# Attention and mixer kernel: three pairs' keys and queries sent ahead of the branch, weight parts in DRAM in rows of 2 KB, and new figures in the planner

## The chip, the cores and the metric

The kernel runs on one core of a Trainium2 chip. The metric is the device time of one execution in microseconds. The kernel before takes 676.57 us (median of three runs, 676.33 to 677.78).

## The reference

Four batches of eight heads, 768 positions, head size 64; each position attends to four sink positions and to a window of 128. The heads' outputs, joined to 512 columns, go through a low-rank mix over positions (U and V, rank 32) and a feed-forward layer of 512 to 2048 to 512 columns. U, V and the two weights are float64.

```python
scores = scale * np.matmul(q, k.transpose(0, 1, 3, 2))
keep = is_sink | in_window
scores = np.where(keep, scores, -1000000000.0)
a = np.exp(scores - np.max(scores, axis=-1, keepdims=True))
a = a / (np.sum(a, axis=-1, keepdims=True) + 1e-09)
x = np.matmul(a, v)                      # joined over the heads to (batch, 768, 512)
h = x.transpose(0, 2, 1) @ U @ V
u = x + h.transpose(0, 2, 1)
out = u + np.maximum(u @ w_ch1, 0.0) @ w_ch2
```

## The kernel before

**Order.** The class `Fast` records every piece of work as a step with an engine (or several to choose from), a duration, what it reads and writes, and a priority. `Plan.order` (L321) lays these steps out in time with a list scheduler (`forward`, L419), corrects the priorities from the end (`backward`, L382), repeats that 40 times and keeps the best order. The steps are then issued engine by engine in that order; an engine works its own list strictly in turn, and so does SP, which issues nearly all DMAs. The figures of the planner are constants at the head of the file: `SWITCH` is what it charges PE for going between matmuls on quarter or half tiles and whole ones, `LAND` the time from a DMA's data to its use, `BACKLOG` the time from which the DMA queues count as busy. No step moves during a run; a wrong figure shows as a wait.

**Beginning.** Before the branch on the window's size (`tc.If`, L1671) the kernel makes masks and constants and sends first transfers: keys (two pieces each) and the first half of the queries of `NFIRST` pairs (L1649 to L1653), and the float64 words of U, of both halves of V and of the first weight tile, into the tiles `big0` to `big3` (L1656 to L1658). `load` (L713) leaves out what is already sent, and `narrow` (L635) takes a `big` tile from the list `early` as long as there is one.

**Attention of batch 0.** Four pairs of heads, in two halves of 384 positions each. For one half of one pair: score matmuls on quarter tiles (PE, L746), folding and adding the mask with the row minimum (DVE, L754 and L759), exponentials with sums (ACT, L762), normalising (POOL or ACT, L783 and L780), transposes (PE, L801), copies and masking of the transposed tiles `oph` (ACT, DVE, POOL, L807 to L812), matmuls with v (PE, L843). Scores take two or four of the eight PSUM banks. Three slots hold keys and queries (`kp`, `qp`); the fourth pair uses space of a weight tile (`own`).

**Feed-forward.** float64 words of a weight come into a `big` tile and are joined to float32 by six steps on DVE, ACT and POOL (`join_steps`, L136 to L144), then split into a high and a low part. Batch 0 uses them from SBUF (L1063 to L1065, L1085) and writes the parts to DRAM: `wd` (three of the four 128x128 corners, L694) and `ws` (four sums of corners, L1130). Batches 1 to 3 work with seven products of halves (`ffn_joint`, L1214, matmuls at L1229) and read one corner or one sum at a time back into a tile `w` or `spare` (`weights`, L1247). In DRAM a row of `wd` holds, for one partition, both halves d with three corners each:

```python
self.wd = [[self.dram(f"wd{j}_{i}", [P, 2, 3, 2 * P], F32R) ...
self.put(wd, lambda ...: (f32(wd())[:, d], f32(w())[:, d, :3]), 3 << 17, at, ...
wa = lambda layer, j, o: lambda i: (..., lambda: self.wd[layer][i]()[:, :, CORNER[...]])
```

so a corner is read as two rows of 1 KB for each partition and a half is written as one row of 3 KB. `stage` and `shrink` share out tiles that batch 0 no longer needs to the work of the later batches.

Of the kernel before, what the change touches and what calls it, by code (L numbers as in the profile page):

```python
# [21 lines left out]
P = 128  # L22
# [12 lines left out]
CH = 384  # L35
# [11 lines left out]
SWITCH = 0.2  # L47
TOGETHER = 2
HOLD = 3.0
BACKLOG = -1.0  # L50
LAND = 1.5
# [7 lines left out]
NFIRST = 2  # L59
# [30 lines left out]
def f32(ap):  # L90
    return ap.bitcast(F32)
# [192 lines left out]
class Plan:  # L284
# [56 lines left out]
    def strained(self):  # L341

        todo = {e: [] for e in self.SYNC}
        for s in sorted(self.steps, key=lambda s: (s.start, s.n)):
            todo[s.eng].append(s)
        left, ready = {}, dict.fromkeys(self.steps, 0.0)
        for s in self.steps:
            left[s] = left.get(s, 0) + len(s.deps) + len(s.after)
            for h in s.heirs:
                left[h] = left.get(h, 0) + 1  # L350
        at, free, tiled = dict.fromkeys(todo, 0), dict.fromkeys(todo, 0.0), False
        dma, port, owner = BACKLOG, 0.0, None
        for _ in self.steps:
            best = None
            for e, q in todo.items():
                if at[e] < len(q) and not left[q[at[e]]]:
                    s = q[at[e]]
                    t = max(free[e], ready[s])
                    if s.ways[e][2] and owner != e:
                        t = max(t, port)  # L360
                    if best is None or t < best[0]:
                        best = t, e, s
            t, e, s = best
            at[e] += 1
            free[e] = t + s.ways[e][0] + STRAIN.get(e, 0.0)
            if e == "PE":
                free[e] += SWITCH * (s.tiled != tiled)
                tiled = s.tiled
            if s.ways[e][2]:
                port, owner = free[e], e  # L370
            end = free[e] + s.lat
            if e == "SP":
                dma = max(dma, free[e] + 0.65) + s.lat
# [45 lines left out]
    def forward(self):  # L419
        avail = dict.fromkeys(self.SYNC, 0.0)  # L420
        ready = {e: [] for e in avail}
# [39 lines left out]
        while done < len(self.steps):  # L461
# [83 lines left out]
class Fast:  # L545
# [3 lines left out]
    def __init__(self, tc, ctx, mask, folds, tri, ident, kept, pairs, early, join, q, k, v, vs, U, V, w1, w2, out):  # L549
        self.tc, self.nc, self.ctx = tc, tc.nc, ctx  # L550
        self.mask, self.folds, self.tri, self.ident = mask, folds, tri, ident
        self.kept, self.flats, self.early, self.join = kept, pairs, list(early), join
# [76 lines left out]
    def put(self, box, pair, nbytes, prio, r=(), part=None, rows=P, slack=0.0):  # L629
        def fn():  # L630
            d, s = pair()
            self.nc.sync.dma_start(d, s)
        self.plan.add("SP", 0.5 if rows == P else 0.65, fn, r=r, w=((box, part),) if box else (), lat=nbytes / 330e3, prio=prio).slack = slack

    def narrow(self, src, n, prio, flat=None):  # L635

        raw, A, T = self.raw(), self.nr(), self.nt()
        if len(self.early) > 0:
            self.early.pop(0)
            self.plan.add("SP", 0.0, lambda: None, w=(raw,), lat=P * n * 8 / 330e3, prio=-1e9)  # L640
        else:
            self.put(raw, lambda: (raw().bitcast(U16)[:, 1:4 * n + 1], src), P * n * 8, prio - 8.0, slack=SLOW)
# [33 lines left out]
    def weights(self, f, prio):  # L676
# [8 lines left out]
        for layer, src in enumerate((self.w1, self.w2)):  # L685
            w, wd, sums = ws[layer], self.wd[layer][i], self.ws[layer][i]
            for d in range(2):
# [6 lines left out]
                self.put(wd, lambda w=w, wd=wd, d=d: (f32(wd())[:, d], f32(w())[:, d, :3]), 3 << 17, at,  # L694
# [18 lines left out]
    def load(self, b, pair, half, t0):  # L713
# [8 lines left out]
        if not early:  # L722
            self.put(qr, lambda: (qr()[:, :q1 - q0], self.q[b, pair][:, q0:q1]), (q1 - q0) * 512, t0 - 15)
        if half != 1:
# [92 lines left out]
    def values(self, parts, t0, vr, xT):  # L817
# [28 lines left out]
        add("PE", 1.2 if len(outs) == 1 else 1.95, run, r=[vr] + [t for _, _, tops in outs for t in tops] + [(xT, half) for half, _, _ in outs],  # L846
# [272 lines left out]
    def prepare(self, tb, tw, ws, d, prio):  # L1119
# [10 lines left out]
        self.put(ws, lambda: (f32(ws())[:, d], f32(t())), 1 << 19, prio, r=each + [(t, 4)], part=d)  # L1130

    def shrink(self):

        keep = lambda g, n, shape: self.over([self.later(g, i, shape, F32) for i in range(n)])
        if self.rest is None:
            self.rest = self.kp, self.qp, self.vp
            self.big = self.over([self.later(g, NRAW - 1, [DM], F32) for g in self.rest])
# [7 lines left out]
    def stage(self, bigs, nts):  # L1145
# [6 lines left out]
        units = [self.again((self.big.boxes[i::3][-1],), g.name, NRAW - 1, [2, CH]) for i, g in enumerate((kp, qp, vp))]  # L1152
# [61 lines left out]
    def ffn_joint(self, b, prio):  # L1214
# [92 lines left out]
        def gather(banks, to, out=None):  # L1307
# [8 lines left out]
            :, :, CORNER[(j, o) if layer == 0 else (o, j)]])  # L1316
        wc = lambda layer, k: lambda i: (self.ws[layer][i], lambda: self.ws[layer][i]()[:, :, k])
# [52 lines left out]
    def run(self):  # L1370
# [6 lines left out]
        self.wd = [[self.dram(f"wd{j}_{i}", [P, 2, 3, 2 * P], F32R) for i in range(NF // 2)] for j in range(2)]  # L1377
        self.ws = [[self.dram(f"ws{j}_{i}", [P, 2, 4, 2 * P], F32R) for i in range(NF // 2)] for j in range(2)]
# [5 lines left out]
        self.wtiles, self.banks, self.bigs, self.accs = {}, [], list(self.early), []  # L1384
# [249 lines left out]
def sink_attention_mixer(ctx, tc, q, k, v, vs, limits, U, V, w1, w2, out):  # L1634
# [5 lines left out]
    with tc.tile_pool(name="idle", bufs=1, space=PSUM) as idle, tc.manual_schedule():  # L1640
# [107 lines left out]
```

## Time and profile before

| | us |
|---|---|
| median of three runs (lowest, highest) | 676.57 (676.33, 677.78) |
| the profiled execution | 674.64 |
| its span, first to last instruction | 672.9 |
| PE busy | 648.1 |
| VectorE (DVE) busy | 530.1 |
| ScalarE (ACT) busy | 420.5 |
| GpSimd (POOL) busy | 256.2 |

The span is that of one profiled execution; its time is that of the span and what lies around it. Busy times are shares of one engine's row. A line number is that of the kernel before. A bracket such as [3.86 <-POOL p L783] behind an instruction gives the idle time of its engine just before it and what ended that.

### The profile page before, as it was taken

To read this page: it belongs to the slowest core of one execution; us is meant where nothing else is said; L and a number is where in the kernel's file an instruction comes from. 1 tells how busy PE (TensorE), PEld (TensorE's weight loads), DVE (VectorE), ACT (ScalarE), POOL (GpSimd) and SP (SyncE) were. 2 spreads that over 40 slices of the span, in tenths; PEclk is the share of its full clock that TensorE was granted. 3 is DMA by queue.
4 is the path that set the end of the run, shared out by engine and by line. 5 is a ranking of instruction groups with operands and counts; after the bars stand their busy time and mean duration, and the time that the engine had idled before them with its cause. 6 is when DMAs were issued, how large, how long until landed. Compare 5 with 4: busy or idle time off the path is not lost.

```text
span 672.9 us, 15525 instructions
## 1 busy us (share of the span) xinstructions
PE 648.1 (96%) x5302; PEld 596.7 (89%) x5302; DVE 530.1 (79%) x1473; ACT 420.5 (62%) x1180; POOL 256.2 (38%) x330
## 2 busy tenths in 40 slices
PE   5998999999999999999999999999999999999996
PEld 4776788888888888889979989999999999999996
DVE  5899999999999788789799799846736964673383
ACT  6988788788674378666578875345436525543551
POOL 3652263454536247365267672231203201120120
PEclk8999999999999999999999999999999999999999
DMA  8459899899778789998898956899888899888883
GB/s 317 132 169 342 310 405 352 327 330 329 275 266 323 253 283 356 375 327 260 297 326 296 354 179 200 267 381 284 243 258 255 265 304 359 263 248 257 253 261 106
DMA packets 134104, 191.57 MB, mean 285 GB/s; under 512 B 10240, under 2 KB 103808, under 8 KB 134016
## 3 DMA queue, kind: packets, MB, share of 16 engines
q1 hardware_dynamic: 133728, 190.10, 84.2%
q8 instruction: 44, 0.72, 0.4%
q14 instruction: 44, 0.36, 0.2%
q10 hardware_dynamic: 288, 0.39, 0.2%
HBM read 141.17 MB, written 49.28 MB: 283 GB/s over the span
## 4 chain that ended last, share of the span: by engine, by line
PE 69%; DVE 16%; DMA 8%; ACT 2%; POOL 2%; issue 2%; SPq 0%; DVEq 0%; POOLq 0%; ACTq 0%
PE bank L1229 45%; PE bank L1085 7%; PE bank L746 3%; DMA ws<-spare 3%; PE bank L843 3%; PE bank L1063 2%; PE bank L1065 2%; PE bank L1064 2%; DVE w L624 2%; DMA w<-wd 2%; PE bank L801 2%; DVE p L759 1%; DVE spare L624 1%; DVE nt L142 1%; ACT p L762 1%
## 5 line engine op out<-in xcount | busy, mean ns | idle before, releaser
L1229 PE MATMUL bank<-w,w 128*128 128x384 f32 x678 | 130.9, 338 | 0.0
L1229 PEld LDWEIGHTS bank<-w,w 128*128 128x128 f32 x678 | 118.4, 188 | 2.4 <-issue 1.4
L762 ACT ACTIVATE p<-p,mn 128x132 f32<-128x132 f32 x192 | 75.5, 397 | 16.5 <-DVE mn L759 16.5
L1229 PE MATMUL bank<-w,spare 128*128 128x384 f32 x342 | 65.0, 336 | 0.0
L1085 PE MATMUL bank<-w,hh 128*128 128x512 f32 x192 | 62.2, 404 | 1.0 <-ACT w L617 0.6
L1234 DVE TENSOR_TENSOR big<-bank,big 128x384 f32<-128x384 f32 x84 | 44.6, 553 | 21.2 <-PE bank L1229 21.0
L626 POOL TENSOR_TENSOR w<-uh,w 128x384 fp32r<-128x384 f32 x22 | 23.0, 1046 | 98.6 <-ACT w L617 74.5
L1229 PEld LDWEIGHTS bank<-w,spare 128*128 128x128 f32 x342 | 60.0, 188 | 0.0
L626 POOL TENSOR_TENSOR spare<-spare 128x128 f32<-128x128 f32 (+1 forms) x53 | 37.5, 717 | 48.2 <-DMA ws<-spare 21.8
L759 DVE CUSTOM_DVE_ANT_0 p<-bank,mask 128x132 f32<-128x132 f32 x192 | 48.0, 287 | 0.1
L809 POOL TENSOR_SCALAR_AFFINE_SELECT oph<-oph 128x320 f32<-128x320 f32 x48 | 28.9, 613 | 46.6 <-ACT oph L617 44.6
L1063 PE MATMUL bank<-ul,w 128*128 128x384 f32 x128 | 43.9, 343 | 0.9 <-DVE ul L624 0.9
L617 ACT CAST w<-ul 128x384 fp32r<-128x384 f32 x56 | 28.8, 515 | 25.4 <-PE bank L1229 22.3
L624 DVE TENSOR_TENSOR spare<-spare 128x128 f32<-128x128 f32 (+1 forms) x87 | 35.8, 433 | 9.7 <-DMA ws<-spare 8.1
L1065 PE MATMUL bank<-uh,w 128*128 128x384 f32 x128 | 43.0, 336 | 0.0
L1064 PE MATMUL bank<-uh,w 128*128 128x384 f32 x128 | 43.0, 336 | 0.0
L746 PE MATMUL bank<-kp,qp 64*64 64x196 f32 (+2 forms) x840 | 39.4, 318 | 3.4 <-DMA qp<-in_q_dram 2.0
L1229 PE MATMUL bank<-spare,w 128*128 128x384 f32 x204 | 41.7, 340 | 0.7 <-DVE ul L1234 0.6
L1085 PEld LDWEIGHTS bank<-w,hh 128*128 128x128 f32 x192 | 34.2, 188 | 8.3 <-issue 2.9
L624 DVE TENSOR_TENSOR w<-ul,w 128x384 fp32r<-128x384 f32 x55 | 32.9, 605 | 8.7 <-ACT w L617 8.5
L617 ACT CAST w<-uh 128x384 fp32r<-128x384 f32 x55 | 28.2, 514 | 18.5 <-PE bank L1229 17.5
L812 POOL TENSOR_SCALAR_AFFINE_SELECT oph<-oph 128x384 f32<-128x384 f32 x64 | 39.2, 636 | 1.0 <-ACT oph L617 0.8
(276 smaller groups left out, 1699.0 us busy)
## 6 DMA issues: line engine op xcount, KB each, us to landing
w<-ws SPq DMA_DIRECT2D x132, 256.0 KB, 4.4
w<-wd SPq DMA_DIRECT2D x102, 256.0 KB, 4.7
big<-in_w_dram SPq DMA_DIRECT2D x32, 512.0 KB, 6.0
ws<-spare SPq DMA_DIRECT2D x32, 512.0 KB, 5.8
spare<-ws SPq DMA_DIRECT2D x60, 256.0 KB, 3.9
wd<-w SPq DMA_DIRECT2D x32, 384.0 KB, 5.9
spare<-wd SPq DMA_DIRECT2D x42, 256.0 KB, 4.0
vp<-in_v_dram SPq DMA_DIRECT2D x15, 384.0 KB, 5.5
```

Of the source, the lines that this page charges most:

```text
L617: return self.plan.any({"ACT": (act(n) + (0.0 if psum else 0.07), lambda: nc.scalar.copy(dst(), src()), False), "DVE": (dve(n) if psum els ...
L624: ways = {"DVE": (dve(n), lambda: nc.vector.tensor_tensor(dst(), a(), b(), op), pool)}
L626: ways["POOL"] = (gps(n), lambda: nc.gpsimd.tensor_tensor(dst(), a(), b(), op), True)
L746: nc.tensor.matmul(st()[a * G:(a + 1) * G, x * TW + to:x * TW + to + wd], qr()[at, q0:q0 + G], kr()[at, k0:k0 + wd], start=True, stop=True ...
L759: add("DVE", dve(SW), lambda st=st, x=x, j=j, part=part, at=at: nc.vector.tensor_tensor_reduce(part(), st()[:, x * TW + half * G:x * TW + ...
L762: add("ACT", act(SW) + 0.22, lambda part=part, at=at: nc.scalar.activation(part(), part(), AF.Exp, bias=at(mn), scale=-1.0, accum_out=at(sm)),
L1063: nc.tensor.matmul(ph()[:, :CH], wh, ul()[:, c, :], start=n == 0, stop=False)
L1064: nc.tensor.matmul(ph()[:, :CH], wl, uh()[:, c, :], start=False, stop=False)
L1065: nc.tensor.matmul(ph()[:, :CH], wh, uh()[:, c, :], start=False, stop=n == NC - 1)
L1085: nc.tensor.matmul(acc[k](), a()[:, sl], w()[:, :, at, m:m + P].rearrange("p d o j -> p o d j"), start=not begin and i == 0 and j == 0, st ...
L1229: nc.tensor.matmul(bank()[:, :CH], w()[:, at:at + P], u()[:, d, :] if n > 1 else u(), start=first and i == 1, stop=last and i == 3 * n, sk ...
L1234: add("DVE", dve(CH), lambda: nc.vector.tensor_tensor(x(), bank()[:, :CH], t(), ALU.add), r=(bank,) if t is x else (bank, t), w=(x,), prio ...
```

## The change

Three things are changed. First, `NFIRST` is 3, so keys and first queries of three pairs are sent before the branch; v of pair 0 is sent there too, and of the float64 words only U (`NEARLY` is 1). The other `big` tiles still exist and are filled behind the branch. Second, `wd` and `ws` are laid out with the corner ahead of the half, so that a corner is one row of 2 KB for each partition when it is read, and three or four rows of 1 KB when a half is written. Third, the planner's figures are others, it lets SP begin 1.6 us after the other engines, and it counts the early transfers as landing one after the other from `BACKLOG` on. Beside these, `shrink` and `stage` hand out the third slots of keys and queries, one tile `uh` and the rest of the `uh` and `ul` tiles for other uses in the later batches.

```diff
-SWITCH = 0.2
+SWITCH = 0.1
-BACKLOG = -1.0
-LAND = 1.5
+BACKLOG = -4.0
+LAND = 1.3
+RATE = 370e3
+BEGIN = 1.6
-NFIRST = 2
+NFIRST = 3
+NEARLY = 1
...
         avail = dict.fromkeys(self.SYNC, 0.0)
+        avail["SP"] = BEGIN
...
-                dma = max(dma, t + s.dur + 0.65) + s.lat
+                dma = max(dma, t + s.dur + 0.65 if s.dur else dma) + s.lat
...
-        self.plan.add("SP", ..., lat=nbytes / 330e3, prio=prio).slack = slack
+        self.plan.add("SP", ..., lat=nbytes / RATE, prio=prio).slack = slack
+    def landing(self, box, nbytes):
+        self.plan.add("SP", 0.0, lambda: None, w=(box,), lat=nbytes / RATE, prio=-1e9).slack = -1.5
...
-                self.put(wd, lambda w=w, wd=wd, d=d: (f32(wd())[:, d], f32(w())[:, d, :3]), 3 << 17, at,
+                self.put(wd, lambda w=w, wd=wd, d=d: (f32(wd())[:, :, d], f32(w())[:, d, :3]), 3 << 17, at,
...
-            if not early:
+            if early:
+                self.landing(kr, NB * SW * 512)
+            else:
                 self.put(kr, lambda: (kr(), self.k[b, pair]), NB * SW * 512, t0 - 16)
...
+        if early and pair == 0:
+            self.landing(vr, NB * 65536)
+        elif half != 1:
             self.put(vr, lambda: (vr(), self.v[b, pair]), NB * 65536, t0 - 8)
...
-        add("PE", 1.2 if len(outs) == 1 else 1.95, run, ...
+        add("PE", 1.2 if len(outs) == 1 else 2.15, run, ...
...
-        self.put(ws, lambda: (f32(ws())[:, d], f32(t())), 1 << 19, prio, r=each + [(t, 4)], part=d)
+        self.put(ws, lambda: (f32(ws())[:, :, d], f32(t())), 1 << 19, prio, r=each + [(t, 4)], part=d)
...
-            :, :, CORNER[(j, o) if layer == 0 else (o, j)]])
-        wc = lambda layer, k: lambda i: (self.ws[layer][i], lambda: self.ws[layer][i]()[:, :, k])
+            :, CORNER[(j, o) if layer == 0 else (o, j)]])
+        wc = lambda layer, k: lambda i: (self.ws[layer][i], lambda: self.ws[layer][i]()[:, k])
...
-        self.wd = [[self.dram(f"wd{j}_{i}", [P, 2, 3, 2 * P], F32R) ...
-        self.ws = [[self.dram(f"ws{j}_{i}", [P, 2, 4, 2 * P], F32R) ...
+        self.wd = [[self.dram(f"wd{j}_{i}", [P, 3, 2, 2 * P], F32R) ...
+        self.ws = [[self.dram(f"ws{j}_{i}", [P, 4, 2, 2 * P], F32R) ...
...
+        kept["vp", 0] = pre.tile([P, 2, NB, D], F32, name="vp0")
+        nc.sync.dma_start(kept["vp", 0], v[0, 0])
...
-        for src, n in ((U, NB * RANK), (V[0], VC), (V[1], VC), (w1[ORDER[0]], DM))[:NBIG]:
+        for src, n in ((U, NB * RANK), (V[0], VC), (V[1], VC), (w1[ORDER[0]], DM))[:NEARLY]:
```

PE at its beginning, before: the end of the scores of pair 1 (keys kp_85), the transposes of pair 0's probabilities, and the first scores of pair 2 (kp_223). A name's number tells buffers apart.

```order
L746 MATMUL bank_183<-kp_85,qp_86 64x196
L746 MATMUL bank_184<-kp_85,qp_86 64x196
L801 MATMUL bank_177<-ident,p_225 128x128 x3
L801 MATMUL bank_178<-ident,p_225 128x128 x3
L746 MATMUL bank_179<-kp_223,qp_236 64x128
L746 MATMUL bank_180<-kp_223,qp_236 64x128
L746 MATMUL bank_179<-kp_223,qp_236 64x68
```

The same place after: pair 1 is kp_85, pair 2 is kp_90, pair 3 is own_224, the probabilities of pair 0 are p_221.

```order
L760 MATMUL bank_187<-kp_85,qp_86 64x196
L760 MATMUL bank_188<-kp_85,qp_86 64x196
L760 MATMUL bank_181<-kp_90,qp_91 64x128
L760 MATMUL bank_182<-kp_90,qp_91 64x128
...
L760 MATMUL bank_183<-kp_90,qp_91 64x196
L760 MATMUL bank_184<-kp_90,qp_91 64x196
L815 MATMUL bank_185<-ident,p_221 128x128 x3
L815 MATMUL bank_186<-ident,p_221 128x128 x3
L760 MATMUL bank_187<-own_224,qp_81 64x128
```

The scores of pair 2 now stand between those of pair 1 and the transposes of pair 0; before, they stood behind them.

SP's list before, from the early transfers past the branch to the fourth pair's and the third pair's data:

```order
L1652 DMA kp_85<-in_k_dram 128x528
L1658 DMA big_94<-in_U_dram 128x768
L1658 DMA big_96<-in_V_dram 128x1536
L1658 DMA big_98<-in_V_dram 128x1536
L1658 DMA big_100<-in_w_dram 128x2048
...
L1671 COMPARE_AND_BRANCH
L632 DMA own_201<-in_k_dram 128x792
L632 DMA vp_203<-in_v_dram 128x768
L632 DMA vp_209<-in_v_dram 128x768
L632 DMA kp_223<-in_k_dram 128x792
L632 DMA qp_236<-in_q_dram 128x384
L632 DMA qp_81<-in_q_dram 128x384
```

And after:

```order
L1671 DMA kp_85<-in_k_dram 128x528
L1671 DMA kp_90<-in_k_dram 128x264
L1671 DMA kp_90<-in_k_dram 128x528
L1674 DMA vp_95<-in_v_dram 128x768
L1679 DMA big_101<-in_U_dram 128x768
...
L1693 COMPARE_AND_BRANCH
L637 DMA own_224<-in_k_dram 128x792
L637 DMA qp_81<-in_q_dram 128x384
L637 DMA qp_86<-in_q_dram 128x384
...
L637 DMA big_103<-in_V_dram 128x1536
L637 DMA big_104<-in_V_dram 128x1536
L637 DMA big_105<-in_w_dram 128x2048
```

Keys of pair 2 and v of pair 0 have moved ahead of the branch (its queries are issued by ACT there); both halves of V and the first weight tile have moved behind the transfers of pair 3 and of the other v.

ACT behind the branch, before: exponentials of pairs 0 (p_225) and 1 (p_252), the normalising of both by three scalings each, the copies of pair 0's transposed tiles (oph), and then pair 2 (p_332).

```order
L769 ACTIVATE r<-sm 128x6
L762 ACTIVATE p_252,sm<-p_252,mn 128x132 x3
L780 ACTIVATE p_225<-p_225,r 128x132 x3
L762 ACTIVATE p_252,sm<-p_252,mn 128x132 x2
L617 COPY oph_290<-bank_177 128x6x64
L769 ACTIVATE r<-sm 128x6
L617 COPY oph_305<-bank_178 128x6x64
L780 ACTIVATE p_252<-p_252,r 128x132 x3
L789 COPY psink<-p_252 128x2x3x4
L762 ACTIVATE p_332,sm<-p_332,mn 128x132 x6
L617 COPY oph_382<-bank_180 128x6x64
```

After, with pair 0 as p_221, pair 1 as p_262 and pair 2 as p_290:

```order
L783 ACTIVATE r<-sm 128x6
L776 ACTIVATE p_262,sm<-p_262,mn 128x132 x5
L776 ACTIVATE p_290,sm<-p_290,mn 128x132
L783 ACTIVATE r<-sm 128x6
L776 ACTIVATE p_290,sm<-p_290,mn 128x132
L622 COPY oph_322<-bank_185 128x6x64
L794 ACTIVATE p_262<-p_262,r 128x132 x3
L622 COPY oph_344<-bank_186 128x6x64
L776 ACTIVATE p_290,sm<-p_290,mn 128x132 x3
L622 COPY oph_378<-bank_183 128x6x64
```

Pair 2's exponentials are now spread between the scalings and copies of pairs 0 and 1; before, they stood behind all of these. Pair 0's scaling is no longer ACT's (POOL has both halves of it).

## Rows read from the trace of the kernel before

**Rows 1.** Busy times of the page: span, then engines.

```profile
span 672.9 us, 15525 instructions
PE 648.1 (96%) x5302; PEld 596.7 (89%) x5302; DVE 530.1 (79%) x1473; ACT 420.5 (62%) x1180; POOL 256.2 (38%) x330
```

**Rows 2.** Windows: length, busy time of each engine (instructions), TensorE clock, DMA share, GB/s.

```profile
0.00:10.00 10.00, 6.19 (x72) 5.44 (x72) 6.47 (x40) 4.76 (x20) 2.97 (x15) 1.00 0.73 261
10.00:20.00 10.00, 5.69 (x68) 4.83 (x68) 4.68 (x35) 7.33 (x34) 3.12 (x5) 0.66 0.95 355
60.00:70.00 10.00, 8.40 (x42) 6.83 (x40) 10.00 (x21) 8.95 (x19) 3.50 (x3) 1.00 1.01 381
7.00:17.00 10.00, 4.15 (x62) 3.23 (x58) 5.16 (x37) 8.14 (x38) 4.26 (x7) 0.74 1.04 403
42.00:58.90 16.90, 14.56 (x99) 9.25 (x98) 15.67 (x33) 12.65 (x27) 2.37 (x5) 1.00 0.69 220
70.00:640.00 570.00, 563.88 (x4556) 525.77 (x4557) 451.86 (x1200) 354.02 (x966) 219.76 (x267) 1.00 0.88 296
450.00:640.00 190.00, 190.00 (x1091) 190.00 (x1090) 113.61 (x219) 94.31 (x194) 33.79 (x32) 1.00 0.87 274
```

**Rows 3.** Timeline of PE, beginning: start, length, instruction, idle time before it.

```profile
6.02 2.44 PE L746 MATMUL bank<-kp,qp 64*64 64x128 f32 x56 [1.42 <-DMA kp<-in_k_dram]
12.32 1.54 PE L801 MATMUL bank<-ident,p 128*128 128x128 f32 x6 [3.86 <-POOL p L783]
15.85 2.26 PE L746 MATMUL bank<-kp,qp 64*64 64x128 f32 x28 [1.99 <-DMA qp<-in_q_dram]
```

**Rows 4.** Chain of waits: start, length, what the end waited for.

```profile
9.43 6.29 DMA qp<-in_q_dram
265.52 6.99 DMA w<-wd
```

**Rows 5.** Timeline of DVE and ACT, 15.4 to 18.5 us.

```profile
17.48 0.50 DVE L754 COPY_PREDICATED bank<-now,bank 128x128 f32<-128x128 int32 x2 [2.52 <-PE bank L746]
18.21 0.41 ACT L762 ACTIVATE p<-p,mn 128x132 f32<-128x132 f32 x1 [2.58 <-DVE mn L759]
```

**Rows 6.** Groups of ACT, 7.8 to 60 us: busy time, mean ns, idle before.

```profile
L780 ACT ACTIVATE p<-p,r 128x132 f32<-128x132 f32 x15 | 5.0, 406 | 0.3 <-DVE r L772 0.3
L617 ACT COPY xT<-bank 128x384 f32<-128x384 f32 x7 | 3.4, 479 | 0.0
```

**Rows 7.** Timeline of PE at the feed-forward's start and at 272 and 289 us.

```profile
63.41 0.45 PE L1063 MATMUL bank<-ul,w 128*128 128x384 f32 x1 [0.24 <-DVE ul L624]
69.42 0.50 PE L1085 MATMUL bank<-w,hh 128*128 128x512 f32 x1 [0.64 <-ACT w L617]
272.65 0.41 PE L1229 MATMUL bank<-qp,w 128*128 128x384 f32 x1 [1.10 <-DMA w<-wd]
289.52 1.31 PE L1229 MATMUL bank<-hl,w 128*128 128x384 f32 x6 [0.21 <-DMA w<-wd]
```

**Rows 8.** DMA queues from 60 to 110 us, then from 400 to 640 us.

```profile
DMA packets 7245, 18.37 MB, mean 367 GB/s; under 512 B 808, under 2 KB 808, under 8 KB 7238
q1 hardware_dynamic: 7238, 18.29, 96.4%
DMA packets 64699, 65.50 MB, mean 273 GB/s; under 512 B 4071, under 2 KB 64165, under 8 KB 64677
q1 hardware_dynamic: 64677, 65.22, 85.8%
```

**Rows 9.** DMA, 250 to 300 us: queue; issues with KB each, median us to landing.

```profile
q1 hardware_dynamic: 11847, 17.72, 102.8%
w<-ws SPq DMA_DIRECT2D x15, 256.0 KB, 6.0
ws<-spare SPq DMA_DIRECT2D x7, 512.0 KB, 6.3
w<-wd SPq DMA_DIRECT2D x14, 256.0 KB, 5.9
```

More of the change, by code (lines that the diff above doesn't have):

```diff
@@ L351, in strained @@
         at, free, tiled = dict.fromkeys(todo, 0), dict.fromkeys(todo, 0.0), False
+        free["SP"] = BEGIN
         dma, port, owner = BACKLOG, 0.0, None
@@ L372, in strained @@
             if e == "SP":
[L373 removed]
+                dma = max(dma, free[e] + 0.65 if s.dur else dma) + s.lat
                 end = dma + LAND + s.slack
@@ L545, with __init__ @@
 class Fast:
-    def __init__(self, tc, ctx, mask, folds, tri, ident, kept, pairs, early, join, q, k, v, vs, U, V, w1, w2, out):
+    def __init__(self, tc, ctx, mask, folds, tri, ident, kept, pairs, bigs, join, q, k, v, vs, U, V, w1, w2, out):
         self.tc, self.nc, self.ctx = tc, tc.nc, ctx
         self.mask, self.folds, self.tri, self.ident = mask, folds, tri, ident
-        self.kept, self.flats, self.early, self.join = kept, pairs, list(early), join
+        self.kept, self.flats, self.stock, self.early, self.join = kept, pairs, bigs, bigs[:NEARLY], join
         self.q, self.k, self.v, self.vs = q, k, v, vs
@@ L632, in fn @@
             self.nc.sync.dma_start(d, s)
-        self.plan.add("SP", 0.5 if rows == P else 0.65, fn, r=r, w=((box, part),) if box else (), lat=nbytes / 330e3, prio=prio).slack = slack
+        self.plan.add("SP", 0.5 if rows == P else 0.65, fn, r=r, w=((box, part),) if box else (), lat=nbytes / RATE, prio=prio).slack = slack
+    def landing(self, box, nbytes):
+        self.plan.add("SP", 0.0, lambda: None, w=(box,), lat=nbytes / RATE, prio=-1e9).slack = -1.5
     def narrow(self, src, n, prio, flat=None):
@@ L639, in narrow @@
             self.early.pop(0)
-            self.plan.add("SP", 0.0, lambda: None, w=(raw,), lat=P * n * 8 / 330e3, prio=-1e9)
+            self.landing(raw, P * n * 8)
         else:
@@ L845, in run @@
                 begun.add(pa)
-        add("PE", 1.2 if len(outs) == 1 else 1.95, run, r=[vr] + [t for _, _, tops in outs for t in tops] + [(xT, half) for half, _, _ in outs],
+        add("PE", 1.2 if len(outs) == 1 else 2.15, run, r=[vr] + [t for _, _, tops in outs for t in tops] + [(xT, half) for half, _, _ in outs],
             w=[pa for _, pa, _ in outs], prio=t0, tiled=True)
@@ L1136, in shrink @@
             self.rest = self.kp, self.qp, self.vp
-            self.big = self.over([self.later(g, NRAW - 1, [DM], F32) for g in self.rest])
+            self.big = self.over([self.later(g, NRAW - 1, [n], F32, lambda t: t[:, :DM]) for g, n in zip(self.rest, (NB * SW, S, DM))])
             self.kp, self.qp = keep(self.kp, NRAW - 1, [NB * SW]), keep(self.qp, NRAW - 1, [S])
@@ L1158, in stage @@
         units += [self.again(last, "spare", 0, [4, 2, CH], F32R, lambda t, o=o: t[:, o]) for o in range(4)]
+        units[10:10] = [self.later(self.uh, 0, [4, CH], F32R, lambda t, o=o: t[:, 2 * o:2 * o + 2]) for o in range(2)]
         self.px, self.flat = (self.over([((get.boxes[x::len(get.slots)][-1],), make) for x, (side, make) in enumerate(get.slots)
@@ L1161, in stage @@
         self.uc = self.over(units)
-        self.raws = self.over([self.later(g, i, [4, CH], F32, o) for g in (self.uh, self.ul) for i in range(2) for o in cuts(4)])
+        self.raws = self.over([
+            self.again((self.big.boxes[i::3][-1],), g.name, NRAW - 1, [n], F32, lambda t, o=o: t[:, o * CH:(o + 1) * CH])
+            for i, (g, n) in enumerate(((kp, NB * SW), (qp, S))) for o in range(2)] + [
+            self.later(g, i, [4, CH], F32, o) for g, i in ((self.uh, 1), (self.ul, 0), (self.ul, 1)) for o in cuts(4)])
         self.a3 = self.over([wt(i, DM, 2 * S) for i in range(3)] + [wt(3, DM, o * DM) for o in range(4)])
@@ L1672, in sink_attention_mixer @@
         with ExitStack() as fctx:
-            Fast(tc, fctx, masks.m, (masks.now, masks.past), tri, ident, kept, pairs, early, join,
+            Fast(tc, fctx, masks.m, (masks.now, masks.past), tri, ident, kept, pairs, bigs, join,
                  q, k, v, vs, U, V, w1, w2, out).run()
```

17 lines of the change are left out of this document (10 added, 7 removed).

## The prediction

> **What bounds the kernel now.** I read the busy times first: PE is busy for 648.1 of 672.9 us, DVE for 530.1, ACT for 420.5 [rows 1]. A busy PE is not PE at its peak, so I looked next at the stretches. From 450 to 640 us PE has no idle time at all, and in the first ten microseconds, the second ten, and the ten from 60 us on it has 3.8, 4.3 and 1.6 us [rows 2]. From about 70 us on the kernel is a nearly unbroken row of matmuls; what an edit saves there is worth nothing unless it takes away idle time of PE or the work of PE itself, and no edit here takes away matmuls. So the end moves with two things only: the moment at which the feed-forward stage of batch 0 starts, and PE's idle time behind it.
>
> The third view is PE's timeline of the beginning [rows 3]. PE does the scores of pairs 0 and 1 at 6.02 us for 2.44 us, then waits 3.86 us for POOL's normalised probabilities of pair 0, transposes them, and waits 1.99 us more for the queries of pair 2. The chain of waits names the same transfer: the queries of pair 2, issued at 9.43 us, land 6.29 us later [rows 4]. The two engines that attention loads most stand still for it: DVE for 2.52 us before 17.48, ACT for 2.58 us before 18.21 [rows 5]. In all of 7 to 17 us DVE is busy for 5.16 of 10 us; from 42 to 58.9 us it is busy for 15.67 of 16.90, and ACT for 12.65 [rows 2]. So there is room at the beginning on both, little on DVE afterwards, some on ACT.
>
> **Term A, three pairs ahead of the branch.** The diff puts k and the first half of q of pair 2, and v of pair 0, among the transfers sent before the branch, and takes V and the first weight tile out of them. In PE's new order pair 2's 14 score matmuls stand ahead of the transposes of pair 0, where PE now idles for 3.86 us. These 28 passes took 2.26 us at a clock that was 0.66 on average in that stretch [rows 2, 3], so they fit in the gap. The data is there: k and q of pairs 0 and 1 (2 x (396 + 192) KB = 1.2 MB) had landed by 6.02 us, and 588 KB more at the 261 GB/s that the queues moved in the first 10 us [rows 2] is 2.3 us, so 8.3 at the latest, while PE finishes pair 1 at 8.46. SP still issues eight transfers and the small one of the limits before the branch; ACT issues a third for q, while it has nothing else to do, so neither costs anything. Behind the branch the first transfer is k of pair 3; ahead of it then stand three pairs, v of pair 0 and U, 2.4 MB, and with it 2.8 MB; at that rate it lands near 12 us, before PE is done with the transposes of pair 0, which end at 13.9 us now [rows 3]. The other wait, 1.99 us for the queries of pair 2, goes for that reason, and pair 3's scores come next, not late for data.
>
> What is late next is ACT. With pair 2 in hand ACT need not stop at 15.6; its 2.58 us of idle time is what the start gives back if ACT is the limit: I take A = -2.6 us. The upper end is both waits of PE in full, 3.86 + 1.99 = -5.9 us. The lower end comes from the new order: up to the copy of t, ACT gets one more scaling of three (1.0 us: 5.0 us for 15 pieces), one more oph copy, two more pair512 copies and two fewer xT copies [rows 6]. An xT copy of 384 columns takes 0.48 us, an oph copy is as long, and one of 512 columns is an estimated 0.48 x 4/3 = 0.64; so +1.0 + 0.5 + 1.2 - 1.0. That is 1.7 us more on ACT, so in the worst case A = -2.6 + 1.7 = -0.9 us. I stay near -2.6, since ACT has 4.3 us of idle time from 42 to 58.9 us to take that load, and since DVE loses four multiplications by tri and two copies of 512 columns in exchange.
>
> V and the first weight tile land later than before; they hide behind attention, for in DVE's new order the first step on V stands behind the softmax of five of the eight half-pairs. If that cover were gone the first feed-forward matmuls would wait; they wait now 0.64 us for a weight cast [rows 7], and I leave it so.
>
> **Term B, pieces of 2 KB.** A weight part read back is now 128 rows of 2 KB where it was 256 of 1 KB; written, it is 384 or 512 rows of 1 KB where it was 128 of 3 or 4 KB. What a packet size costs is read from two stretches [rows 8]: from 400 to 640 us, where 64165 of 64699 packets are below 2 KB, 65.22 MB took 85.8% of the engines, 65.22 / (240 x 0.858) = 317 GB/s for a full share; from 60 to 110 us, with 808 of 7245 below 2 KB, it is 18.29 / (50 x 0.964) = 379 GB/s. So a small piece costs a sixth more. It matters only where the queues are full: from 250 to 300 us, with a share of 102.8% [rows 9]. There 29 parts of 256 KB (7.6 MB) fall from 24.0 to 20.0 us of full share, and 7 writes of 512 KB (3.7 MB) rise from 9.7 to 11.6, together -2.1 of 51. PE's longest wait for a weight part in that stretch is 1.10 us, behind a chain piece of 6.99 us [rows 4, 7]. Two microseconds less in the queues over the stretch should take that wait: B = -1.1 us. Ends: -1.3 (that and the 0.21 before 289.52 us go) and +1.1 (another of its size comes, because the plan now believes that data lands 0.2 us sooner and at 370 instead of 330 GB/s, and so puts its consumer closer). From 450 us on a lower share than 0.87 buys nothing: PE is busy all the time [rows 2].
>
> By the Trainium skill, "DMA: Bandwidth & Descriptors", section Specifications, 512 B is the smallest transfer at line rate; by that rule 1 KB rows lose nothing, and B would be 0 instead of -1.1, with a sum of -2.6. The rows just named disagree with it, 317 against 379 GB/s.
>
> **Term C, the plan.** New figures (a tile switch of 0.1 instead of 0.2, the values matmuls 2.15 instead of 1.95, BACKLOG, LAND, RATE, BEGIN) make the planner draw the whole order anew; nothing is added on an engine, but each order has its own small waits. PE's idle time from 70 to 640 us is 570 - 563.9 = 6.1 us [rows 2]. I take C = 0, with ends of -2.5 (about four tenths of it go) and +2.5 (as much comes). The last stage keeps its sums and stores.
>
> **Sum.** -2.6 - 1.1 + 0 = -3.7 us. The profiled execution took 674.64 us (span 672.9 and 1.7 around it), so 670.9 there; the median of the three runs shown is 676.57, 1.9 above, and the prediction is for that: 676.57 - 3.7 = 672.9 us.
>
> **The rivals.** (1) The gain of the start is spent before the feed-forward stage. For it: DVE is busy for 10.00 of the 10 us from 60 to 70, when PE idles for 1.6; if DVE's row of casts and joins sets when the first weights are ready, and these now get their data later, pairs that are done sooner only wait longer. Against it: DVE's idle time of 4.8 us from 7 to 17 us is what would be filled, so its row too comes earlier. Then only B is left: 676.57 - 1.1 = 675.5 us.
> (2) More than ACT's pause is won: PE's two waits go whole and the join steps move up with them. A = -5.9, B = -1.1: 669.6 us. For it: DVE's empty half of 7 to 17 us. Against: ACT is busy for 8.14 of these 10 us and gets more to do.
> (3) Slower: weight parts come late in the joint stages. The place is the matmuls that wait for w or spare from wd and ws, above all between 250 and 330 us; the price is 1.1 us each, as before 272.65. The plan's thinner margin speaks for it, with landings of 5.9 to 6.0 us there [rows 9], and also the small rows in which parts are now written while the queues are full. From the third new wait on (2.6 / 1.1 = 2.4) it decides over A. Should one in five of the 29 loads of that stretch be late, 6 x 1.1 - 2.6 = +4.0 us: 680.6 us. Against it: the reads get shorter, and PE idles 6.1 us in all behind 70 us, for every cause together.
> (4) The change of size does nothing, as where the queues have room: B = 0, 674.0 us; it has the sign of the forecast and is held in its case.
>
> **How the numbers follow.** The forecast with its neighbours (671 to 674.5) 0.54, rival 1 0.20, rival 2 0.15, rival 3 0.11. What this kernel's measurement tells from no change is 0.2%, 1.35 us: faster is below 675.2, slower above 677.9. Nearly all of the forecast and rival 2, and a quarter of rival 1, are faster: 0.73. Most of rival 1 and a little of the forecast are the same: 0.17. Rival 3 is slower: 0.10. For the range I add the distances from the sum to the ends as independent ones: below 3.3, 0.2 and 2.5, together 4.1; above 1.7, 2.2 and 2.5, together 3.7. So 668.8 to 676.6, and with a little more above for rival 3, 677.0.
>
> **What the new profile would show.** A is right if PE does three pairs of scores without a wait from about 6 to 10 us, if no wait for qp stands before 20 us, if ACT has no pause above 1 us between 8 and 20 us, and if the first matmul of the feed-forward stage (63.41 us now [rows 7]) comes 2 to 4 us sooner. B is right if the share of the queues from 400 to 640 us falls from 85.8% toward 73% and PE no longer waits a microsecond for w from wd. C is right if PE's idle time from 70 to 640 us stays between 3.6 and 8.6 us. The prediction is wrong if the first feed-forward matmul stays at 63 us, or if waits for w, spare or the joins of weights add more than 2.5 us to PE behind 70 us.

## The result and the profile after

The changed kernel takes 681.73 us (median of six runs, 680.44 to 682.43); the kernel before took 677.40 beside it (676.33 to 678.82). The ratio is 1.0061, 95% interval [1.0044, 1.0077]: slower by 4.3 us, where 672.9 was predicted. The profiled execution took 681.97 us, 0.2 us above its kernel's median; that of the kernel before took 674.64 us, 2.8 below its. So the two profiles lie 3 us further apart than the two kernels do. The busy times, beside [rows 1]:

```profile
span 680.2 us, 15557 instructions
PE 651.1 (96%) x5302; PEld 599.2 (88%) x5302; DVE 535.6 (79%) x1464; ACT 427.8 (63%) x1185; POOL 261.3 (38%) x336
```

The span grew by 7.3 us. PE issues as many matmuls as before, but is busy for 3.0 us more, and idle for 4.3 more. The windows of the changed kernel, beside [rows 2] (length, busy time of PE, PEld, DVE, ACT and POOL, granted clock, DMA share, GB/s), say where:

```profile
0.00:70.00 70.00, 57.94 (x592) 44.58 (x593) 62.75 (x241) 54.81 (x192) 31.97 (x61) 0.98 0.75 257
10.00:20.00 10.00, 7.23 (x115) 5.62 (x114) 8.57 (x68) 10.00 (x48) 7.48 (x14) 1.00 0.97 345
70.00:640.00 570.00, 558.11 (x4513) 519.86 (x4512) 449.92 (x1182) 358.79 (x966) 223.21 (x270) 1.00 0.87 291
450.00:640.00 190.00, 190.00 (x1085) 189.74 (x1084) 117.44 (x227) 94.61 (x195) 36.54 (x35) 1.00 0.85 271
312.00:314.00 2.00, 2.00 (x11) 1.91 (x10) 0.56 (x1) 0.87 (x3) 1.72 (x4) 0.50 0.05 17
314.00:316.00 2.00, 2.00 (x10) 2.00 (x9) 0.67 (x2) 0.82 (x3) 0.16 (x1) 0.69 0.05 8
```

And the one row of the kernel before that the first of these is held against, the same view:

```profile
0.00:70.00 70.00, 56.37 (x587) 43.38 (x587) 57.82 (x235) 55.45 (x194) 30.29 (x57) 0.95 0.71 244
```

From 70 to 640 us PE now idles for 570 - 558.11 = 11.9 us instead of 6.1, so +5.8; up to 70 us it idles for 12.06 instead of 13.63, so -1.6. From 450 us on it still has no idle time. From 10 to 20 us DVE is busy for 8.57 us where it was 4.68, and ACT for all of it: the start does what the change says. The last two rows are the second cost: in these four microseconds PE is busy throughout, but at a granted clock of 0.50 and 0.69, which loses (0.50 + 0.31) x 2 = 1.6 us. The start gains about as much: over the first 70 us the mean granted clock was 0.95 and is 0.98, and over the whole span it is 0.993 in both profiles.

PE's timeline (start, length, instruction, idle time before it) has the signs of the start, beside [rows 3, 7], and below them the six waits for weight parts:

```profile
5.95 4.21 PE L760 MATMUL bank<-kp,qp 64*64 64x128 f32 x84 [1.35 <-DMA kp<-in_k_dram]
12.66 0.55 PE L815 MATMUL bank<-ident,p 128*128 128x128 f32 x3 [2.50 <-DVE mn L773]
13.97 1.24 PE L760 MATMUL bank<-own,qp 64*64 64x128 f32 x28
62.62 0.45 PE L1077 MATMUL bank<-ul,w 128*128 128x384 f32 x1 [1.18 <-DVE ul L629]
68.75 0.62 PE L1099 MATMUL bank<-w,hh 128*128 128x512 f32 x2
...
243.12 0.42 PE L1247 MATMUL bank<-p,w 128*128 128x384 f32 x1 [0.68 <-DMA w<-wd]
250.31 0.42 PE L1247 MATMUL bank<-w,w 128*128 128x384 f32 x1 [0.99 <-DMA w<-wd]
310.60 0.77 PE L1247 MATMUL bank<-hh,w 128*128 128x384 f32 x3 [2.33 <-DMA w<-ws]
342.84 0.79 PE L1247 MATMUL bank<-uh,w 128*128 128x384 f32 x3 [0.66 <-DMA w<-ws]
416.70 0.58 PE L1247 MATMUL bank<-w,w 128*128 128x384 f32 x2 [0.92 <-DMA w<-ws]
433.30 0.42 PE L1247 MATMUL bank<-spare,w 128*128 128x384 f32 x1 [1.55 <-DMA w<-ws]
```

Three pairs of scores now run in one piece (84 passes), and pair 3 (`own`) starts without a wait. But the first feed-forward matmul comes only 0.8 us sooner than before (62.62 for 63.41), the first of the second layer 0.7 (68.75 for 69.42). The six waits are 7.1 us in sum. The list of PE's waits from 70 to 640 us (line, what it waited for: us, times, longest) says what remains beside them:

```profile
PE bank L1247 <- DMA w<-ws: 5.5, 4, 2.3
PE bank L1077 <- DVE hl L1088: 1.7, 1, 1.7
PE bank L1247 <- DMA w<-wd: 1.7, 2, 1.0
PE bank L1247 <- DVE w L629: 1.4, 1, 1.4
```

The chain of waits shows the landings behind the two longest DMA waits, beside [rows 4] (start, length, what landed):

```profile
302.49 7.97 DMA w<-ws
428.20 4.96 DMA w<-ws
```

The first lands 0.14 us before PE starts at 310.60; it was issued at 302.49. DVE's and ACT's longest pauses, which were 2.52 and 2.58 us [rows 5], are 1.21 (from 10 to 20 us) and 0.70 (from 8 to 20 us), in their timelines:

```profile
14.91 0.49 DVE L768 COPY_PREDICATED bank<-now,bank 128x128 f32<-128x128 int32 x2 [1.21 <-PE bank L760]
8.12 0.41 ACT L776 ACTIVATE p<-p,mn 128x132 f32<-128x132 f32 x1 [0.70 <-DVE mn L773]
```

Last the queues, beside [rows 8, 9], first from 400 to 640 us and then from 250 to 300 us (packets; queue with packets, MB and share; issues, KB each, median us to landing):

```profile
DMA packets 35745, 64.04 MB, mean 267 GB/s; under 512 B 3965, under 2 KB 8061, under 8 KB 35722
q1 hardware_dynamic: 35722, 63.74, 82.9%
...
q1 hardware_dynamic: 11493, 18.13, 101.9%
w<-ws SPq DMA_DIRECT2D x17, 256.0 KB, 5.9
w<-wd SPq DMA_DIRECT2D x14, 256.0 KB, 5.4
```

From 400 to 640 us packets below 2 KB fell from 64165 to 8061, yet the share fell only from 85.8 to 82.9%, with 2% fewer bytes: a full share still moves 63.74 / (240 x 0.829) = 320 GB/s, after 317.

### The profile page after: what moved, and what is told of

Its sections match the earlier page's. It is cut to its first block, busy times and chain, and to the rows that moved or that the text cites. A ratio compares the mean times of both kernels' runs of the same rounds, so it can differ in the third digit from the quotient of the medians.

```text
span 680.2 us, 15557 instructions
## 1 busy us (share of the span) xinstructions
PE 651.1 (96%) x5302; PEld 599.2 (88%) x5302; DVE 535.6 (79%) x1464; ACT 427.8 (63%) x1185; POOL 261.3 (38%) x336
## 4 chain that ended last, share of the span: by engine, by line
PE 76%; DVE 10%; DMA 8%; ACT 2%; issue 1%; POOL 0%; SPq 0%; DVEq 0%; POOLq 0%; ACTq 0%
PE bank L1247 48%; PE bank L1099 6%; PE bank L760 4%; PE bank L857 4%; DMA w<-ws 3%; PE bank L815 3%; PE bank L1077 2%; PE bank L1079 2%; PE bank L1078 2%; DMA w<-wd 2%; DVE nt L145 1%; DVE spare L146 1%; DMA ws<-spare 1%; DVE ul L629 1%; PE bank L964 1%
## 5 line engine op out<-in xcount | busy, mean ns | idle before, releaser
L1247 PE MATMUL bank<-w,w 128*128 128x384 f32 x792 | 154.6, 339 | 3.5 <-DVE w L629 1.4
L1247 PEld LDWEIGHTS bank<-w,w 128*128 128x128 f32 x792 | 138.2, 188 | 7.1 <-DVE w L629 1.8
L1247 PE MATMUL bank<-w,spare 128*128 128x384 f32 x348 | 67.1, 338 | 0.0
L1247 PEld LDWEIGHTS bank<-w,spare 128*128 128x128 f32 x348 | 61.6, 188 | 0.1
L1099 PE MATMUL bank<-w,hh 128*128 128x512 f32 x192 | 61.4, 401 | 0.0
L629 DVE TENSOR_TENSOR spare<-spare 128x128 f32<-128x128 f32 (+1 forms) x93 | 39.0, 444 | 10.1 <-DMA ws<-spare 5.8
L631 POOL TENSOR_TENSOR spare<-spare 128x128 f32<-128x128 f32 (+1 forms) x47 | 30.1, 650 | 42.2 <-DMA ws<-spare 15.8
L823 POOL TENSOR_SCALAR_AFFINE_SELECT oph<-oph 128x320 f32<-128x320 f32 x51 | 27.3, 548 | 36.3 <-ACT oph L622 35.6
L1099 PEld LDWEIGHTS bank<-w,hh 128*128 128x128 f32 x192 | 34.5, 188 | 6.8 <-issue 1.4
L797 POOL TENSOR_TENSOR p<-p,r 128x396 f32<-128x396 f32 x32 | 27.9, 879 | 31.4 <-DVE r L786 19.9
L1247 PEld LDWEIGHTS bank<-spare,w 128*128 128x128 f32 x210 | 36.8, 188 | 3.2 <-ACT nt L622 1.8
```

Of the source, the lines that this page charges most:

```text
L629: ways = {"DVE": (dve(n), lambda: nc.vector.tensor_tensor(dst(), a(), b(), op), pool)}
L631: ways["POOL"] = (gps(n), lambda: nc.gpsimd.tensor_tensor(dst(), a(), b(), op), True)
L1099: nc.tensor.matmul(acc[k](), a()[:, sl], w()[:, :, at, m:m + P].rearrange("p d o j -> p o d j"), start=not begin and i == 0 and j == 0, st ...
L1247: nc.tensor.matmul(bank()[:, :CH], w()[:, at:at + P], u()[:, d, :] if n > 1 else u(), start=first and i == 1, stop=last and i == 3 * n, sk ...
```

## The experiments

Four theories stand in the expectations. D: the reads of weight parts that come late cost the lost time. W: the small rows of the writes delay them. M: the new `LAND` and `RATE` let the planner put reads too close to their use. L: every newly drawn order is a draw with its own small waits, wherever they fall, and this one is a bad one. Each run was timed beside the kernel before on its chip, and each ratio is to that; intervals are 95%.

### One part at a time: e1, e2, e3, e4

e1 is the kernel before with the new layout alone, in the same order:

```diff
-self.dram(f"wd{j}_{i}", [P, 2, 3, 2 * P], F32R)
+self.dram(f"wd{j}_{i}", [P, 3, 2, 2 * P], F32R)
```

(and `ws` likewise). 

> The kernel before with wd and ws alone laid out in rows of 2 KB; its order is the old one. Theory M (margin: the new figures for landing time and rate place the loads of weight parts too close to their use) and theory L (lot: any new order has its own waits, whatever the figures): 0 to 1.3 us faster than before, since the one wait of 1.10 us for w from wd shrinks; DMA share from 450 to 640 us falls from 0.87 to about 0.75. Theory W (the writes in rows of 1 KB delay the loads): slower by 2 us or more, with new waits for w between 200 and 330 us.

Measured: 675.47 us, ratio 0.9972 [0.9955, 0.9989], so -1.9 us. Its waits for `w` from `wd`, in the list of PE's waits from 70 to 640 us, are 0.9 us in sum; before they were 1.3:

```profile
PE bank L1229 <- DMA w<-wd: 0.9, 2, 0.6
```

W falls: with small writes and the old order the kernel is a little faster. The profile doesn't hold all of the gain: the span is 672.5 us after 672.9, and PE's idle time behind 70 us 5.5 after 6.1. Nor did the queues empty as expected: from 450 to 640 us their share is 0.86 after 0.87, where 0.75 was expected. Since the order is the old one, e1 also prices the rows by themselves. Its queues from 400 to 640 and from 60 to 110 us, beside [rows 8]:

```profile
DMA packets 36726, 65.55 MB, mean 273 GB/s; under 512 B 4075, under 2 KB 8171, under 8 KB 36704
q1 hardware_dynamic: 36704, 65.27, 84.5%
DMA packets 10086, 18.43 MB, mean 369 GB/s; under 512 B 811, under 2 KB 4979, under 8 KB 10081
q1 hardware_dynamic: 10081, 18.37, 99.9%
```

In the first stretch, where nearly all rows grew from 1 to 2 KB, a full share moves 65.27 / (240 x 0.845) = 322 GB/s after 317. In the second, where the writes of `wd` now make half of the packets small, it moves 18.37 / (50 x 0.999) = 368 after 379. So the size of the rows is worth 2 to 3% of the queues here.

e2 is the kernel before with the planner's figures alone (also `BEGIN` and the new count of `dma`; the figures are put on one line here):

```diff
-SWITCH = 0.2, BACKLOG = -1.0, LAND = 1.5, 330e3, 1.95
+SWITCH = 0.1, BACKLOG = -4.0, LAND = 1.3, 370e3, 2.15
```

> The kernel before with the planner's new figures alone (switch 0.1, landing 1.3, rate 370, backlog -4, values 2.15, SP beginning at 1.6); the same transfers and layouts as before. Theory M: slower by 3 to 7 us, 680 to 684, and PE waits for w or spare from wd and ws behind 200 us sum to 4 us or more. Theory L: anywhere within 4 us of before, and its waits need not be for weight parts. Theory W: as before.

Measured: 680.05 us, 1.0030 [1.0005, 1.0055]. PE idles for 8.7 us from 70 to 640 us. But the list of its waits there has no weight part among its four longest:

```profile
PE bank L976 <- DVE xhl L626: 2.0, 2, 1.4
PE bank L1231 <- DVE w L626: 1.5, 1, 1.5
PE bank L1231 <- DVE mn L761: 1.4, 1, 1.4
PE bank L1231 <- ACT uh L1279: 1.2, 1, 1.2
```

The new figures do make a worse order here, but through DVE and ACT. The time is at the edge of what M asked for (680 to 684 us), but M asked for waits on transfers.

e3 is the changed kernel with the layout and the figures set back (so the start, `landing` and `BEGIN` alone):

```diff
-SWITCH = 0.1, BACKLOG = -4.0, LAND = 1.3, RATE = 370e3, 2.15
+SWITCH = 0.2, BACKLOG = -1.0, LAND = 1.5, RATE = 330e3, 1.95
```

> The changed kernel with the old layout of wd and ws and the old figures (switch 0.2, landing 1.5, rate 330, backlog -1, values 1.95); three pairs ahead, v of pair 0 ahead and SP's beginning at 1.6 stay. Theory M: the start's 1.4 to 2 us are kept and no wait for a weight part is above 1.1 us, 675 to 676. Theory L: the start's gain plus or minus 4 us. Theory W: 675 to 676.

Measured: 676.31 us, 0.9976 [0.9959, 0.9993], -1.6 us. Idle time behind 70 us is 6.3 us.

e4 is the kernel before with a change that means nothing, to see what another order is worth. `SLACK` is a margin for what PE waits for:

```diff
-SLACK = 0.0344
+SLACK = 0.0354
```

> The kernel before with one figure of the planner moved by a thousandth of a microsecond that means nothing on the chip (SLACK 0.0354 instead of 0.0344): a new draw of the order. Theory M: within 1.4 us of before. Theory L: off by more than 1.4 us to either side, with PE's idle time from 70 to 640 us off its 6.1 us by as much.

Measured: 672.61 us, 0.9932 [0.9910, 0.9953], -4.6 us. PE idles for 2.75 us from 70 to 640 us, in the same windows:

```profile
70.00:640.00 570.00, 567.25 (x4591) 531.24 (x4590) 443.47 (x1191) 370.48 (x992) 220.09 (x270) 1.00 0.90 299
```

One thousandth of a microsecond in the plan moves the time by more than any part of the change did. That is L.

### Do the late reads cost it? e5, e6

e5 is the changed kernel in the same order, where the reads into seven of the slots (234 of 336 reads by the trace, 7 more than the expectation counts) fetch 64 KB instead of 256. The rest of such a part is left out, and PE works on what lies there; the number and order of its matmuls stay. The edit, shortened:

```diff
+light = (len(self.a3.boxes) - 1) % len(self.a3.slots) < 7
+if light: self.put(piece, lambda: (f32(piece())[:, :P], f32(view())[:, 0, :P]), ...)
```

> The changed kernel, its order untouched, but 227 of the reads of weight parts bring only the first 128 columns (64 KB of 256 KB), so that part of the computation is left out; the 94 reads into spare stay whole. Theory D (the late reads cost the time): the six waits of PE for w from wd and ws (7.1 us) shrink below 1.5 us and the time falls by 5 to 9 us (the half clock behind the longest of them goes too), to 673 to 677. If those waits are only the place where some other delay shows, they turn into waits for DVE or ACT and the time falls by less than 2 us.

Measured: 672.81 us, 0.9923 [0.9897, 0.9949]. Its busy times, its windows and, apart, its waits from 70 to 640 us:

```profile
PE 647.3 (96%) x5302; PEld 599.3 (89%) x5302; DVE 534.0 (80%) x1464; ACT 428.3 (64%) x1185; POOL 262.1 (39%) x336
70.00:640.00 570.00, 565.24 (x4577) 530.23 (x4576) 454.82 (x1195) 365.42 (x979) 224.17 (x270) 1.00 0.68 218
312.00:314.00 2.00, 2.00 (x14) 2.00 (x13) 2.00 (x6) 0.39 (x2) 1.35 (x2) 1.00 0.15 40
```

```profile
PE bank L1077 <- DVE hl L1088: 2.3, 1, 2.3
PE bank L1247 <- DVE w L629: 1.1, 1, 1.1
```

With the same order the six waits are gone, DVE's two stay, and the clock at 312 us is full. PE's idle time behind 70 us is 4.8 us where it was 11.9, and its busy time is back at 647.3 us. From e5 to the changed kernel is 1.0061 - 0.9923 = 1.4% of 677.4, 9.3 us (about +-2.1 from the two intervals); the six waits and the slow clock were 7.1 + 1.6 = 8.7. D is shown: without the late reads this order would be faster than before. (The start of the profiled e5 had no part in it: its second layer began 1.9 us later than the changed kernel's, at 70.68 us.)

e6 is the changed kernel with the old layout, in the new order. 

> The changed kernel with the old layout of wd and ws alone (reads in rows of 1 KB), its order untouched. From the layout's gain in the old order (677.87 to 675.47) and from full queues: the waits for weight parts grow by 1 to 4 us, 683 to 686. Should the writes in rows of 1 KB be what delays the loads: faster, 678 to 681.

Measured: 682.90 us, 1.0080 [1.0052, 1.0109]. Two of the four waits for `w` from `ws` are gone from its list, the two for `wd` stay:

```profile
PE bank L1247 <- DMA w<-ws: 3.7, 2, 2.1
PE bank L1247 <- DMA w<-wd: 1.2, 2, 0.7
```

The expectation missed: these waits were to grow by 1 to 4 us and are 4.9 us in sum after 7.1, and the time differs from the changed kernel's by less than the intervals. So it is the order that is late, with either size of row; W falls again.

### A margin or a draw? e7 to e15

e7 is the changed kernel with `SLACK` 0.0354, e8 the changed kernel with the two old landing figures:

```diff
-LAND = 1.3
+LAND = 1.5
-RATE = 370e3
+RATE = 330e3
```

> The changed kernel with SLACK 0.0354 instead of 0.0344: a new draw of the order under the new figures. Theory L (any draw has its own waits): off 681.7 by more than 1.4 us, more likely below, 674 to 681, as the old kernel's draw was 5 us off. Theory M (the new figures make every draw bad): 680 to 684, with 4 us or more of waits for weight parts.

> The changed kernel with the old landing time and rate in the planner (1.5 and 330 instead of 1.3 and 370). Theory M: the waits for w from wd and ws fall below 2 us and the time to 674 to 677. Theory L: anywhere from 673 to 683, with waits of any kind.

Measured: e7 675.71 us, 0.9970 [0.9950, 0.9991]; e8 669.23 us, 0.9879 [0.9845, 0.9913]. e8 taken alone speaks for M, whose waits were to go (0.2 us is left), but it is faster than M (674 to 677 us) or L (673 to 683) had it. And e7 keeps the thin margin, and its waits for weight parts are gone as well: one of 0.2 us is left.

```profile
PE bank L1247 <- DMA w<-wd: 0.2, 1, 0.2
```

So more orders were drawn: two each under the new landing figures (e9, e10) and the old ones (e11, e12), then two of the kernel before (e13, e14) and a fourth under the old landing figures (e15). The edits are those of e7 and e8 with other values of `SLACK`.

> The changed kernel with SLACK 0.0334 instead of 0.0344, so another order drawn under the same new figures. Theory M (LAND 1.3 and RATE 370e3 place reads too close): the order again has waits for weight parts, PE idles 8 us or more from 70 to 640 us, 677 us or more. Theory L (every order is a draw with its own waits, and the changed kernel's draw was a bad one): something between 670 and 680 us, no rule for which wait; idle time 3 to 10 us.

> The changed kernel with SLACK 0.0364, a third order under the new figures (beside 0.0344 and 0.0354). M: waits for weight parts of 3 us or more in sum, 677 us or more. L: between 670 and 680 us.

> The changed kernel with the old LAND 1.5 and RATE 330e3 and with SLACK 0.0334: a second order under these two old figures (the first took 669.2 us). M: hardly a wait for weight parts again, 668 to 672 us. L: 670 to 680 us, no better on average than the orders under the new figures.

> The changed kernel with LAND 1.5, RATE 330e3 and SLACK 0.0364: a third order under the two old figures. M: 668 to 672 us, waits for w from wd and ws under 1 us in sum. L: 670 to 680 us.

> The kernel before with SLACK 0.0334: a third order without any part of the change (the others took 677.5 and 672.6 us). Theory L (each order is a draw; the change as a whole moves the typical order by little, some 2 us for the start and the rows): 671 to 681 us, waits on any engine. Theory M (only the new landing figures make bad orders): 672 to 678 us, without waits for weight parts above 2 us in sum.

> The kernel before with SLACK 0.0364: a fourth order without the change. L: 671 to 681 us, so that the four orders of before spread by 5 us or more, as those of the changed kernel do (672.7 to 681.7). M: 672 to 678 us.

> The changed kernel with LAND 1.5, RATE 330e3 and SLACK 0.0354: a fourth order under the old landing figures (the others took 669.2, 673.5 and 674.2 us). L: 669 to 679 us. M: 669 to 674 us, no wait for weight parts above 1 us in sum.

All twelve orders: median in us, ratio; then PE's idle time from 70 to 640 us, and the start of the first second-layer matmul (L1085 or L1099), both from the profiled execution.

| SLACK | kernel before | changed kernel | changed, LAND 1.5 and RATE 330e3 |
|---|---|---|---|
| 0.0334 | e13: 673.85, 0.9960; 3.6; 72.98 | e9: 672.74, 0.9929; 4.8; 67.50 | e11: 673.54, 0.9949; 8.2; 69.41 |
| 0.0344 | 677.40, 1; 6.1; 69.42 | 681.73, 1.0061; 11.9; 68.75 | e8: 669.23, 0.9879; 3.5; 68.17 |
| 0.0354 | e4: 672.61, 0.9932; 2.8; 72.82 | e7: 675.71, 0.9970; 4.8; 69.39 | e15: 671.84, 0.9918; 5.2; 70.65 |
| 0.0364 | e14: 675.49, 0.9962; 8.4; 71.68 | e10: 675.13, 0.9967; 5.5; 67.33 | e12: 674.18, 0.9954; 6.9; 70.13 |
| mean | 0.9964; 5.2; 71.7 | 0.9982; 6.7; 68.2 | 0.9925; 5.9; 69.6 |

Intervals of the last runs: e9 [0.9904, 0.9954], e10 [0.9942, 0.9991], e11 [0.9920, 0.9978], e12 [0.9931, 0.9976], e13 [0.9940, 0.9980], e14 [0.9939, 0.9985], e15 [0.9884, 0.9951]. M in its plain form falls: e9 and e10, with the thin margin, take 672.74 and 675.13 us, where M had 677 or more, and e15, with the thick one, has more wait for `w` from `ws` than e10 (1.3 us against 0.4). e11 and e12, at 673.54 and 674.18 us, lie above M's 668 to 672. L holds: within a column the orders spread by 4.8 to 9.0 us (5 or more were expected of the first, which has the 4.8). Whether the two landing figures shift the mean of the orders is open. The means differ by 0.0057, but the ratios of the middle column spread with a standard deviation of 0.0056, most of it from one order, so four each don't decide. Nor do they show that the change as a whole is a gain: 0.9982 in the middle column is no lower than 0.9964 in the first. The fastest order is e8, 1.2% ahead of before; its interval speaks for that order, and not for its figures.

## Why the prediction was wrong

**Failed: Term C.** It took the new plan at 0 with ends of +-2.5 us, because PE's idle time behind 70 us was 6.1 in all and "about four tenths" seemed a fair swing. The new order's idle time is 11.9, +5.8 us, and the clock at 312 us took 1.6 more; e5 shows that the late reads cost this. The twelve orders range from 2.8 to 11.9 us of idle time. The 6.1 of one trace was no scale for another order: it is what one drawing happened to leave.

**Rival 3 is what happened, at a chance of 0.11.** Its price, 1.1 us for each wait, and its count, six, come close: the six waits are 7.1 us. Its place holds for two of the six, the longest among them; the others stand at 243, 343, 417 and 433 us. Its reason, the thinner margin, is not shown: e2, e7, e9 and e10 have the margin and no such wait of a microsecond. My argument against it, that reads get shorter, counted for little: e6 reads in the old rows and has the same time within the intervals. That the measured 681.73 us lies so near rival 3's 680.6 is luck in part, for the draw set the number of waits. The stated range ended at 677.0 us, below this rival's price.

**Term A, -2.6 us: the start went as reasoned; that its gain reaches the end is not shown.** Three pairs run without a wait, the wait for `qp` is gone, ACT has no pause above 1 us from 8 to 20 us. In the profiled pair the feed-forward stage comes 0.8 us sooner, short of the 2 to 4 that were named as a sign. But one pair can't tell: with the order unchanged, the second layer began at 69.42 us in the execution of before and at 71.57 in e1, and with the new order at 68.75 in the changed kernel, 68.98 in e6 and 70.68 in e5. Over the orders it starts at 71.7 us on average without the change and at 68.2 and 69.6 with it, 2.1 to 3.5 us sooner. Part of that may be the clock, which term A left out: the mean granted clock of the first 70 us is 0.93 to 0.95 in the four orders without the change and 0.95 to 1.00 in the eight with it. From the means, 0.935 against 0.965 and 0.97, times 70 us, I estimate 2 to 2.5 us of it at most, and less where PE waited anyway. At the end the gain can't be seen: the ratios' means are 0.9964 without the change and 0.9982 and 0.9925 with it.

**Term B, -1.1 us: right in sign, wrong in its price.** e1 has -1.9 us [-3.0, -0.7]. But the queues' share was to fall toward 73%; it fell to 82.9, and to 84.5 in e1. I had put the gap between 317 and 379 GB/s [rows 8] down to the size of the rows alone, a sixth. In one and the same stretch and order the rows change the rate by 2 to 3% (322 after 317, 368 after 379), so most of the gap lies in what else differs between the two stretches; what that is stays open. PE's waits for `w` from `wd` lost 0.4 us in e1, not 1.1, so that the number came out near is luck, and where e1's gain lies is not shown. The Trainium skill's rule in "DMA: Bandwidth & Descriptors", section Specifications, that 512 B are enough for line rate, nearly fits these rows (322 after 317), though it gives no reason for e1's gain.

**Rivals 1, 2 and 4.** Rival 1 (the start's gain is spent before the feed-forward stage) is not decided by the profiled pair, since executions of one order differ by as much; the means over the orders speak against it. Rival 2's -5.9 us was not seen. Rival 4 is refuted by e1's time, though closely.

## What to carry to other kernels

Where a planner draws the whole order anew, an edit's own gain of 2 to 4 us can't be read from one order before and one after, nor a price from two different stretches of one kernel; draw some orders of each by a change that means nothing, and compare the groups. Until then give the redrawing a spread as wide as such orders show, here some 5 to 9 us. To see what a late transfer costs, shorten the transfers and leave the order alone.

## What the runs showed of the hardware

The granted clock fell to its lower level (0.50, 1.2 GHz) after PE's wait of 2.33 us before 310.60, and rose again in the window from 314 to 316 us. In e14 it fell as well, after a wait of 2.67 us, in the windows of e14:

```profile
70.00:72.00 2.00, 0.32 (x1) 0.19 (x1) 2.00 (x6) 1.03 (x2) 0.00 (x0) 1.00 0.92 234
72.00:74.00 2.00, 1.53 (x4) 1.13 (x4) 1.93 (x6) 1.22 (x3) 0.00 (x0) 0.51 0.76 252
```

But in e11, whose PE waited for 2.60 us, it did not fall. PE's timeline of e11, and then its windows:

```profile
290.55 1.84 PE L1247 MATMUL bank<-w,w 128*128 128x384 f32 x9 [2.60 <-DVE w L629]
```

```profile
288.00:290.00 2.00, 0.00 (x0) 0.00 (x0) 2.00 (x4) 0.98 (x2) 1.61 (x3) 1.00 1.11 391
290.00:292.00 2.00, 1.45 (x8) 1.46 (x9) 1.58 (x5) 0.10 (x1) 0.00 (x0) 1.00 0.99 341
```

So a wait of that length may cost some 1.6 us more than itself, or nothing more; what decides is open. The other surprise is the start: the same order began the second layer at 69.42 us in the execution of before and at 71.57 in e1, whose queries of pair 2 were waited for 2.75 us instead of 1.99 and whose mean granted clock of the first 70 us was 0.93 instead of 0.95. PE's timeline of e1:

```profile
17.04 2.25 PE L746 MATMUL bank<-kp,qp 64*64 64x128 f32 x28 [2.75 <-DMA qp<-in_q_dram]
```
